# Transposing P for two layers with 40 moving columns and masked evictions

## The chip, the cores and the metric

The kernel runs on one core of a Trainium2 chip, in one launch. The metric is device time in microseconds (us): 2682.25 us is the median of three runs before the change. The engines are TensorE (PE for matmuls, PEld for its weight loads), VectorE (DVE), ScalarE (ACT), GpSimd (POOL) and SyncE (SP).

## The reference

The model is two identical layers, each an attention with a carried memory followed by a gated feed-forward, over 2048 tokens of 576 features, all in bf16:

```
x = x + A(layernorm(x));  x = x + B(layernorm(x));  x = x + A(layernorm(x));  x = x + B(layernorm(x))

A: for each of 64 segments of 32 tokens:
     h = [mem (8 rows), segment (32 rows)]            # 40 rows
     q, k, v = h Wq, h Wk, h Wv                       # 32 heads of 128
     p = softmax(mask(q k^T / sqrt(128)))             # 40 x 40 for each head
     o = (p v) Wo;  mem = o[:8];  out = o[8:]
B: out = (silu(x w1) * (x w3)) w2                     # 4608 wide
```

Each segment needs the memory that the segment before it left, so attention is a chain of 64 steps in each layer.

## The kernel before

**Steps and layers.** The kernel walks 72 steps `t`. At step `t` it does segment `t` of layer 0 and segment `t - 8` of layer 1 (`LAG = 8`). Where both exist (`both(t)`, 56 steps) the two are worked on together: matmuls that use the same weights stream 80 columns, 40 of each layer. The other 16 steps have one layer and 40 columns. `role(t)` is the parity of the step; it decides which layer's columns come first and in which order the rows of keys lie. The feed-forward and the other work of both layers is spread between the steps.

**Groups.** Each step handles the 32 heads in `NG = 4` groups of `GH = 8`; 288 groups in all, 224 of them with two layers. A group runs through these nodes:

- `QK`, `QKt` and their evictions `QKe` (tile `QKT`), then `SC`, the scores of 8 heads. Layer 0's rows stand on partitions 0 to 39, layer 1's on 64 to 103.
- The softmax: DVE adds the mask, takes the maximum and subtracts it, ACT takes the exponential, DVE sums and inverts, and `sm_pb` multiplies and writes P into the tile `PB`. For each head `PB` has the queries on its partitions (0 to 39 and 64 to 103) and 128 columns, one for each row of `V`. `p_at` says which columns a layer's keys take; those of the two layers do not overlap, and the rest is zero.
- `TR` (`ptr`): PE transposes P. `PB[0:104, head]` is the stationary operand, a selection from the identity `ident` the moving one. With two layers the selection has 80 columns, 40 from the partitions of each layer, so 8 heads fill two PSUM banks, 4 heads each.
- `PTe` (`pt_ev`): two evictions, one for each bank, copy the result into the tile `PTS` (128 x 320 each). The planner gives each to ACT or to DVE (`cp` then emits an activation with `Copy` or a `tensor_copy`).
- `pbz` (`pb_zero`): POOL clears `PB` for its next use.
- `PV` (`pv`): for each head the block of `V` is stationary and the head's 80 columns of `PTS` are moving. Then `OTe` evicts into `OT`, and `WO`, `WOt` multiply by the output weights.

There is one `PTS` buffer (`POOLS["pts"]` is 1), two of `PB`, and 8 PSUM banks shared by all.

**Order.** `make_nodes` lists the nodes with durations, dependences and slots; `plan` lays them out. PE's order is not planned: it is the string `ORDER`, one letter for each PE node (`T` is `TR`, `P` is `PV`), whose middle part `FOUR` stands for four steps and is repeated 11 times. In the trace that period is 156.4 us long and holds 16 groups. The order on ACT, DVE and POOL, and which of ACT and DVE takes an eviction (engine `"AD"`), come out of the planned times. Runs of PE nodes share a mode: in `"col"` mode a matmul of 128 weight columns is issued as two of 64, at two column positions of the array, so a `TR` is then 16 matmuls.

**Lines.** All matmuls are recorded at L591, all ACT operations at L594, all DVE operations at L597 and all DMAs of SP at L600, since helpers emit them; POOL's clearing of `PB` is at L1010. Groups in the profile are therefore told apart by their tiles: `bank<-ident,PB` is `TR`, `PTS<-bank` is `PTe`, `bank<-PTS,V` is `PV`.

Of the kernel before, what the change touches and what calls it, by code (L numbers as in the profile page):

```python
# [7 lines left out]
BF = mybir.dt.bfloat16  # L8
F32 = mybir.dt.float32
ACT = mybir.ActivationFunctionType  # L10
ALU = mybir.AluOpType
AX = mybir.AxisListType

P = 128
R64 = 64
# [6 lines left out]
QW = SEG + MEM  # L22
# [5 lines left out]
GH = H // NG  # L28
# [11 lines left out]
def role(t):  # L40

    return (t - LAG) % 2
# [133 lines left out]
def actc(*ns):  # L176

    return sum(max(0.067 + n * 0.000833, 0.19) for n in ns)
# [11 lines left out]
def ew(*ns):  # L190
    return (actc(*ns), dve(*ns))
# [33 lines left out]
class Opt:  # L225

    qk, qkt, sc, tr, pv, wo, wog, vm = 0.0079, -0.0342, 0.0268, 0.1447, 0.0406, 0.2653, 0.0725, 0.1407
# [4 lines left out]
def make_nodes(em, nseg, pools, o=Opt, dma_bw=230e3, load_bw=400e3):  # L232
# [4 lines left out]
    def node(*a, **k):  # L237
        n = Node(*a, **k)
        nodes.append(n)
        return n  # L240

    def banks(n=2):
        return [Slot("bank") for _ in range(n)]
# [22 lines left out]
    b = banks(1)  # L266
# [88 lines left out]
    def step(t):  # L355
        ls = layers_of(t)
        nl = 2 if both(t) else 1
        c80 = 40 * nl
        e = role(t)
        hx = [ht_ready[li, t] for li in ls]  # L360
        hm = ht_mem[t]
        mm80 = max(c80 / 2.4 + 2.5, 25.0) / 1000
        rd = reads_ht.setdefault(t, [])

        for k in () if paired(t) else ((0, 1) if e and both(t) else (0,)):
            last_v[:] = v_nodes("VM", t, k, t + o.vm + 0.01 * k, o.vmt, (lambda k: lambda b, tail: em.vm(t, k, b, tail))(k), em.vm_strips(t, k),
                                hm[:1] + hx + (ld_v if t == 0 else []), hm[1:], {})
        me = steps[t]
        if t == nst - 1:
            last_reads[0].extend(last_v)  # L370
        y = em.ys[t] = Slot("bank", users=2)
        wos, wots = [], []
        for g in range(NG):
            qs, qe = [], []
            for u in (2 * g, 2 * g + 1):
                q = Slot("qkt", users=1)
                b = banks()
                pq = t + o.qk + o.ustep * u
                m_ = node("PE", 32 * mm80, em.qk(t, u, b), deps=hx + hm[:1] + ([ld_h[u // 4]] if t == 0 else []),
                          prio=pq, mode="full", acq=[q] + b, name="QK")  # L380
                n = node("PE", 4 * mm80, em.qk_tail(t, u, b), deps=hx + hm + ([ld_h[u // 4]] if t == 0 else []), prio=pq + o.qkt, mode="row",
                         acq=[q] + b, name="QKt")
                rd += [m_, n]
                me[f"QK{u}"], me[f"QKt{u}"] = m_, n
                for r in (0, 1):
                    qe.append(node("AD", ew(256, 64) if nl == 2 else ew(160), em.qk_ev(t, u, r, q, b[r]), deps=[m_, n], prio=t + o.ustep * u,
                                   rel=[b[r]], name="QKe"))
                qs.append(q)
            s = banks(1)[0]
            sme = Slot("sme")  # L390
            pf = t + o.gstep * g
            sc = node("PE", 8 * (0.0165 * nl if nl == 2 else 0.029), em.scores(t, g, qs, s), deps=qe, prio=pf + o.sc, mode="col" if nl == 2 else "full/col", acq=[s, sme], rel=qs, name="SC")
            a = node("DVE", dve(320), em.sm_add(t, g, s, sme), deps=[sc], prio=pf, rel=[s], name="add")
            m_ = node("DVE", dve(320, 320) + 0.13, em.sm_max(t, g, sme), deps=[a], prio=pf, name="maxsub")
            c = node("ACT", 0.105 + 320 * 0.000833, em.sm_exp(t, g, sme), deps=[m_], prio=pf, name="exp")
            pb = Slot("pb")
            d = node("DVE", dve(320) + 0.2, em.sm_sum(t, g, sme), deps=[c], prio=pf, name="sum")
            w = 0.168 * (4 - e if nl == 2 else 2) + nl * 320 / 960
            pbs = node("DVE", w, em.sm_pb(t, g, sme, pb), deps=[d], prio=pf, acq=[pb], rel=[sme], name="pb")
            pts = Slot("pts")  # L400
            bt = banks()
            tr = node("PE", 8 * mm80, em.ptr(t, g, pb, bt), deps=[pbs], prio=pf + o.tr, mode="full/col", acq=[pts] + bt, name="TR")
            node("POOL", 1.2, em.pb_zero(pb), deps=[tr], prio=pf, rel=[pb], name="pbz")
            pe_ = [node("AD", ew(4 * c80), em.pt_ev(t, g, m, bt[m], pts), deps=[tr], prio=pf, rel=[bt[m]], name="PTe") for m in (0, 1)]
            if paired(t):
                hn = [ht_ready[li, s] for s in (t + 1, t + 2) for li in (0, 1) if (li, s) in ht_ready]
                gb, gd = vg_nodes(t, g, hm[:1] + hx + hn, hm[1:])
                vx_ev["VM", t, g] = vg_out(t, g, gb, gd, R64)
            b = banks()
            ot = Slot("ot")  # L410
            pv = node("PE", 8 * mm80, em.pv(t, g, pts, b), deps=pe_ + vx_ev["VM", t, g] + vx_ev["VX", t - e, g],
                      prio=pf + o.pv, mode="full/col", acq=b + [ot], rel=[pts], name="PV")
            pvs[t, g] = pv
            if paired(t):
                vx_ev["VX", t + 1, g] = vg_out(t, g, gb, gd + [pv], 0)
            ote = [node("AD", ew(4 * c80), em.ot_ev(t, g, ab, b[ab], ot), deps=[pv], prio=pf, rel=[b[ab]], name="OTe") for ab in (0, 1)]
            wo = node("PE", 32 * mm80, em.wo(t, g, ot), deps=ote + ([ld_o[g]] if t == 0 else []), prio=t + o.wo + o.wog * g, mode="full",
                      acq=[y] if g == 0 else [], name="WO")
            wot = node("PE", 4 * mm80, em.wo_tail(t, g, ot), deps=[wo], prio=t + o.wo + o.wog * g, mode="col", rel=[ot], name="WOt")
            if g:  # L420
                wo.after(wos[0])
            if g:
                wot.after(wots[0])
            wos.append(wo)
            wots.append(wot)
            me[f"SC{g}"], me[f"TR{g}"], me[f"PV{g}"], me[f"WO{g}"] = sc, tr, pv, wo
        if t == nst - 1:
            last_reads[1].extend(me[f"{k}{u}"] for u in range(8) for k in ("QK", "QKt"))
        nxt = [li for li in ls if t - LAG * li + 1 < nseg]
        ye = []  # L430
        yo = node("ACT", actc(c80), em.y_odd(t), deps=wots[3:], prio=t - 0.008, name="Yodd")
        if nxt:
            m = 8 * len(nxt)
            ye.append(node("ACT", actc(4 * m), em.y_mem(t, nxt, 0), deps=wos[3:] + wots, prio=t - 0.01, name="Ymem"))
            ye.append(node("DVE", dve(m, m), em.y_mem(t, nxt, 1), deps=[yo] + ye, prio=t - 0.005, name="Ymem"))
        ht_mem[t + 1] += ye
        yts = [node("ACT", actc(*([128] * nl)), em.yts(t, ls, 0), deps=wos[3:] + wots + ye, prio=t + 0.01, rel=[y], name="YTS")]
        yts.append(node("DVE", dve(*([32] * nl)), em.yts(t, ls, 1), deps=[yo] + yts, prio=t + 0.01, rel=[y], name="YTSt"))
        for li in ls:
            yx[li, t - LAG * li] = yts  # L440
# [121 lines left out]
SW = 2 * QW  # L562
# [5 lines left out]
class Emitter:  # L568
# [446 lines left out]
    def ptr(self, t, g, pb, b):  # L1015

        def f(n):
            nq = self.nq(t)
            e = role(t) if nq == SW else 0
            sel = self.T.ident[0:104, R64 * e:R64 * e + QW]  # L1020
            if nq == SW:
                sel = bass.AP(sel.tensor, sel.offset, [list(v) for v in sel.ap][:1] + [[R64, 2], [1, QW]])
            for j in range(GH):
                self.mm(self.bk(b[j // 4])[:, (j % 4) * nq:(j % 4 + 1) * nq], self.T.PB[0:104, pb.i, j, :], sel, True, True)
        return f

    def pt_ev(self, t, g, m, b, pts):
        def f(n):
            w = 4 * self.nq(t)
            self.cp(n, self.T.PTS[:, pts.i, m * w:(m + 1) * w], self.bk(b)[:, 0:w])  # L1030
        return f

    def pv(self, t, g, pts, b):
# [171 lines left out]
def kernel(  # L1205
# [15 lines left out]
    nc = tc.nc  # L1221
# [9 lines left out]
    T = Tiles()  # L1231
    em = Emitter(nc, tc, T, a, nseg)
# [4 lines left out]
    sp = ctx.enter_context(tc.tile_pool(name="state", bufs=1))  # L1237
# [4 lines left out]
    T.WV = wp.tile([P, 9 * H * E // 2], BF, name="WV")  # L1242
    T.WO = wp.tile([P, H, D], BF, name="WO")

    T.ident = sp.tile([P, P + QW], BF, name="ident")

    T.maskb = sp.tile([P, 2, QW], BF, name="maskb")
    T.mhalf = sp.tile([P, 1], F32, name="mhalf")
# [24 lines left out]
    nc.gpsimd.memset(T.ident[:], 0.0)  # L1273
    nc.gpsimd.affine_select(out=T.ident[:, 0:P], in_=T.ident[:, 0:P], compare_op=ALU.not_equal, fill=1.0, base=0,
                            pattern=[[-1, P]], channel_multiplier=1)
    nc.gpsimd.tensor_copy(T.ident[:, P:P + QW], T.ident[:, 0:QW])

    nc.gpsimd.memset(T.maskb[:], 0.0)
    for kd in (0, 1):
        for e in (0, 1):  # L1280
            m = T.maskb[R64 * kd:R64 * kd + QW, e, :]
            x0 = MEM if kd == e else 0
            nc.gpsimd.affine_select(out=m[:, x0:x0 + SEG], in_=m[:, x0:x0 + SEG], compare_op=ALU.is_ge,
                                    fill=MASK_NEG, base=-x0, pattern=[[-1, SEG]], channel_multiplier=1)
# [47 lines left out]
```

## Time and profile before

| | |
|---|---|
| median of three runs | 2682.25 us (2681.96 to 2682.86) |
| profiled execution, first to last instruction | 2684.2 us |
| TensorE clock granted, mean | 0.995 |
| `TR` matmuls, two layers, whole | 1296, busy 73.6 us |
| `TR` matmuls, two layers, half width | 992, busy 30.6 us |
| `PTS` evictions on ACT, 320 elements | 301, mean 436 ns |
| `PTS` evictions on DVE, 320 elements | 147, mean 480 ns |

The profiled execution is one execution; no time of its own is given beside its span, which is 2.0 us above the median of the runs. A row of a group reads: line, engine, operation, tiles written and read, shape, count, then busy time in us and the mean of one in ns, then the idle time of the engine before them and what ended it. Matmuls overlap in the pipeline, so that the mean of one is longer than the step from one to the next.

### The profile page before, as it was taken

Reading aid. Unit: us, or ns where it says so; the run is one execution under the profiler, and the core shown is the slowest. Engines: PE = TensorE matmul, PEld = TensorE weight load, DVE = VectorE, ACT = ScalarE, POOL = GpSimd, SP = SyncE. Lnnn points to the kernel's source line nnn. Section 1 sums busy time; section 2 is a strip of 40 time slices with the busy share of each in tenths; the row PEclk is TensorE's granted clock in tenths of the full one; section 3 lists DMA queues with packets and bytes.
Section 4 is the critical chain, followed back from the end, with each engine's and each line's share of the span. In section 5 each row is a group of like instructions: output and inputs, shape, how many; then the busy total and the mean of one; then the engine's idle time right before and its main releaser. Section 6 shows DMA issues by size and latency. Waiting matters only on the chain.

```text
span 2684.2 us, 136846 instructions
## 1 busy us (share of the span) xinstructions
PE 2621.2 (98%) x60881; PEld 2292.9 (85%) x60933; DVE 2111.8 (79%) x5485; ACT 1346.4 (50%) x3916; POOL 332.2 (12%) x400
## 2 busy tenths in 40 slices
PE   5999999999999999999999999999999999999998
PEld 4888888889888888988888898888889888888887
DVE  4787887887888778787877878787787878687876
ACT  2655554454545455454544545454454545455453
POOL 1111110110111011011101101110110111011110
PEclk8999999999999999999999999999999999999999
DMA  9064524344342434434333443423344342334457
GB/s 319 4 178 118 166 72 125 97 120 118 99 127 84 114 99 119 118 100 126 88 112 97 120 118 100 126 87 113 98 120 118 102 126 82 114 98 130 125 169 256
DMA packets 478178, 322.08 MB, mean 120 GB/s; under 512 B 26024, under 2 KB 467760, under 8 KB 476944
## 3 DMA queue, kind: packets, MB, share of 16 engines
q1 hardware_dynamic: 474048, 305.43, 38.7%
q8 instruction: 477, 7.82, 1.2%
q0 software_dynamic: 3024, 6.93, 0.9%
q10 hardware_dynamic: 512, 0.94, 0.2%
q14 instruction: 117, 0.96, 0.1%
HBM read 308.49 MB, written 2.36 MB: 116 GB/s over the span
## 4 chain that ended last, share of the span: by engine, by line
PE 89%; DMA 3%; DVE 3%; ACT 3%; issue 1%; SPq 1%; ACTq 0%; DVEq 0%
PE bank L591 89%; ACT V L594 1%; SPq L600 1%; DMA W<-in_B_w_dram 1%; DMA W<-in_A_Wk_dram 1%; DVE STAT L597 1%; DVE SME L597 0%; DMA WO<-in_A_Wo_dram 0%; DVE V L597 0%; DVE HTT L597 0%; DVE PB L597 0%; DMA XN<-in_A_x_dram 0%; ACT SME L594 0%; DVE PTS L597 0%; ACT PTS L594 0%
## 5 line engine op out<-in xcount | busy, mean ns | idle before, releaser
L591 PEld LDWEIGHTS <-W 128*128 128x128 bf16 (+2 forms) x32064 | 1267.3, 100 | 118.8 <-issue 55.7
L591 PE MATMUL bank<-HT,W 128*128 128x80 bf16 (+3 forms) x23040 | 807.0, 197 | 14.9 <-ACT HT L594 5.7
L591 PE MATMUL bank<-XTB,W 128*64 128x256 bf16 (+5 forms) x9024 | 664.3, 263 | 4.6 <-DMA W<-in_B_w_dram 3.1
L594 ACT ACTIVATE QKT<-bank 128x256 bf16<-128x256 f32 (+2 forms) x1477 | 343.2, 314 | 362.1 <-PE bank L591 334.1
L1010 POOL MEMSET PB<- 128x1024 bf16 x288 | 273.9, 951 | 1888.4 <-PE bank L591 1537.4
L591 PE MATMUL bank<-OT,WO 128*128 128x80 bf16 (+3 forms) x11520 | 410.9, 198 | 4.6 <-issue 2.0
L591 PEld LDWEIGHTS <-WO 128*128 128x128 bf16 (+1 forms) x11520 | 381.4, 102 | 30.4 <-issue 17.7
L594 ACT ACTIVATE V<-bank 32x512 bf16<-32x512 f32 (+1 forms) x594 | 335.8, 585 | 110.9 <-PE bank L591 104.5
L591 PE MATMUL bank<-WV,HT 128*32 128x512 bf16 (+4 forms) x3628 | 366.2, 383 | 5.5 <-issue 3.2
L591 PE MATMUL bank<-W2C,HTT 128*64 128x288 bf16 (+1 forms) x3040 | 320.1, 287 | 0.8 <-DMA W2C<-in_B_w_dram 0.4
L597 DVE TENSOR_REDUCE STAT<-SME 104x8 f32<-104x320 f32 (+1 forms) x576 | 274.6, 477 | 18.2 <-ACT SME L594 12.4
L597 DVE TENSOR_TENSOR PB<-SME,STAT 40x128 bf16<-40x128 f32 (+4 forms) x912 | 274.9, 335 | 11.3 <-POOL PB L1010 0.5
L594 ACT ACTIVATE HTT<-bank 128x512 bf16<-128x512 f32 (+1 forms) x324 | 177.6, 557 | 196.8 <-PE bank L591 195.5
L591 PEld LDWEIGHTS <-HT 128*32 128x32 bf16 (+4 forms) x3680 | 158.1, 99 | 120.3 <-issue 17.9
L591 PEld LDWEIGHTS <-HTT 128*64 128x64 bf16 (+1 forms) x3104 | 229.4, 104 | 32.1 <-issue 0.6
L597 DVE CAST QKT<-bank 128x128 bf16<-128x128 f32 (+4 forms) x571 | 154.5, 317 | 123.4 <-PE bank L591 122.4
L597 DVE SCALAR_TENSOR_TENSOR XR<-bank,XR 128x288 f32<-128x288 f32 x576 | 239.6, 446 | 13.8 <-PE bank L591 10.9
L597 DVE SCALAR_TENSOR_TENSOR HTT<-HTT,bank 128x512 bf16<-128x512 bf16 (+1 forms) x324 | 202.1, 624 | 56.1 <-ACT HTT L594 51.8
L594 ACT ACTIVATE OT<-bank 128x320 bf16<-128x320 f32 (+1 forms) x425 | 157.0, 405 | 169.5 <-PE bank L591 165.5
L597 DVE TENSOR_TENSOR HTT<-HTT,bank 128x512 bf16<-128x512 bf16 (+1 forms) x324 | 203.6, 628 | 29.0 <-PE bank L591 1.4
L594 ACT ACTIVATE PTS<-bank 128x320 bf16<-128x320 f32 (+1 forms) x395 | 148.2, 404 | 132.3 <-PE bank L591 95.7
L594 ACT ACTIVATE SME<-SME 104x320 f32<-104x320 f32 (+1 forms) x288 | 135.3, 470 | 153.4 <-DVE SME L597 151.1
(61 smaller groups left out, 1837.7 us busy)
## 6 DMA issues: line engine op xcount, KB each, us to landing
W<-in_B_w_dram SPq DMA_DIRECT2D x612, 256.0 KB, 3.7
W2C<-in_B_w_dram SPq DMA_DIRECT2D x306, 288.0 KB, 3.3
W<-in_B_w_dram SPq DMA_DIRECT2D x612, 32.0 KB, 3.3
W<-in_B_w_dram SPq DMA_DIRECT2D x8, 1024.0 KB, 10.5
W<-in_A_Wq_dram SPq DMA_DIRECT2D x9, 512.0 KB, 9.7
WO<-in_A_Wo_dram SPq DMA_DIRECT2D x4, 1152.0 KB, 17.7
XR<-in_A_x_dram POOLq DMA_DIRECT2D x16, 288.0 KB, 3.4
WV<-in_B_w_dram SPq DMA_DIRECT2D x4, 1152.0 KB, 11.3
```

Source lines behind the costliest of these rows:

```text
L591: self.ch("PE", self.nc.tensor.matmul(out, lhsT=lhsT, rhs=rhs, start=start, stop=stop, skip_group_check=True, **k))
L594: self.ch("ACT", self.nc.scalar.activation(*a, **k))
L597: self.ch("DVE", getattr(self.nc.vector, fn_)(*a, **k))
L600: self.ch("SP", self.nc.sync.dma_start(out=out, in_=in_))
L1010: return lambda n: self.ch("POOL", self.nc.gpsimd.memset(self.T.PB[:, pb.i], 0.0))
```

## The change

`TR` no longer selects the two layers into separate columns. Its moving operand is a new constant `fold` of 40 columns, which holds an identity at partitions 0 to 39 and another at 64 to 103. The product has, for each head, 40 columns: column `q` is query `q` of layer 0 plus query `q` of layer 1, on each row of `V`. Since a row of `V` belongs to one layer only, one of the two is always zero.

`PTS` keeps its layout of 80 columns a head. The 8 heads now take 320 columns of one bank, and each of the two evictions reads all of them and writes one half of every head's 80 columns: 8 runs of 40. It multiplies by a 0/1 mask per partition from the new constant `slots`, as the `scale` of the activation on ACT or with `tensor_scalar` on DVE, so that a row of `V` that belongs to the other layer is zero in this half. In steps with one layer the transpose has 40 columns as before, and the two evictions copy a half of the bank each, without a mask.

In the node list `TR` takes one bank with two users in place of two banks, and its planned duration is changed. `fold` and `slots` are built by POOL at the start; a copy of 40 columns behind `ident` goes.

```diff
-            bt = banks()
-            tr = node("PE", 8 * mm80, em.ptr(t, g, pb, bt), deps=[pbs], prio=pf + o.tr, mode="full/col", acq=[pts] + bt, name="TR")
+            bt = Slot("bank", users=2)
+            tr = node("PE", 8 * 0.0258, em.ptr(t, g, pb, bt), deps=[pbs], prio=pf + o.tr, mode="full/col", acq=[pts, bt], name="TR")
             node("POOL", 1.2, em.pb_zero(pb), deps=[tr], prio=pf, rel=[pb], name="pbz")
-            pe_ = [node("AD", ew(4 * c80), em.pt_ev(t, g, m, bt[m], pts), deps=[tr], prio=pf, rel=[bt[m]], name="PTe") for m in (0, 1)]
+            pe_ = [node("AD", ew(4 * c80), em.pt_ev(t, g, m, bt, pts), deps=[tr], prio=pf, rel=[bt], name="PTe") for m in (0, 1)]
...
     def ptr(self, t, g, pb, b):
         def f(n):
-            nq = self.nq(t)
-            e = role(t) if nq == SW else 0
-            sel = self.T.ident[0:104, R64 * e:R64 * e + QW]
-            if nq == SW:
-                sel = bass.AP(sel.tensor, sel.offset, [list(v) for v in sel.ap][:1] + [[R64, 2], [1, QW]])
             for j in range(GH):
-                self.mm(self.bk(b[j // 4])[:, (j % 4) * nq:(j % 4 + 1) * nq], self.T.PB[0:104, pb.i, j, :], sel, True, True)
+                self.mm(self.bk(b)[:, j * QW:(j + 1) * QW], self.T.PB[0:104, pb.i, j, :], self.T.fold[0:104, :], True, True)
         return f
 
     def pt_ev(self, t, g, m, b, pts):
         def f(n):
-            w = 4 * self.nq(t)
-            self.cp(n, self.T.PTS[:, pts.i, m * w:(m + 1) * w], self.bk(b)[:, 0:w])
+            src = self.bk(b)[:, 0:GH * QW]
+            if not self.both(t):
+                w = 4 * QW
+                self.cp(n, self.T.PTS[:, pts.i, m * w:(m + 1) * w], src[:, m * w:(m + 1) * w])
+                return
+            dst = self.T.PTS[:, pts.i, :].rearrange("p (h n) -> p h n", h=GH)[:, :, m * QW:(m + 1) * QW]
+            keep = self.T.slots[:, role(t), m ^ role(t):(m ^ role(t)) + 1]
+            src = src.rearrange("p (h n) -> p h n", h=GH)
+            if n.by == "ACT":
+                self.act(dst, src, ACT.Copy, scale=keep)
+            else:
+                self.v("tensor_scalar", dst, src, keep, None, op0=ALU.mult)
         return f
...
+    nc.gpsimd.memset(T.fold[:], 0.0)
+    for r in (0, R64):
+        nc.gpsimd.affine_select(out=T.fold[:], in_=T.fold[:], compare_op=ALU.not_equal, fill=1.0, base=-r,
+                                pattern=[[-1, QW]], channel_multiplier=1)
+    nc.gpsimd.memset(T.slots[:], 0.0)
+    for e, kd, lo, hi in ((0, 1, 24, 80), (1, 0, 72, 112)):
+        inside, outside = T.slots[:, e, kd:kd + 1], T.slots[:, e, 1 - kd:2 - kd]
...
```

More of the change, by code (lines that the diff above doesn't have):

```diff
@@ L1243 @@
     T.WO = wp.tile([P, H, D], BF, name="WO")
-    T.ident = sp.tile([P, P + QW], BF, name="ident")
+    T.ident = sp.tile([P, P], BF, name="ident")
+    T.fold = sp.tile([P, QW], BF, name="fold")
+    T.slots = sp.tile([P, 2, 2], F32, name="slots")
     T.maskb = sp.tile([P, 2, QW], BF, name="maskb")
@@ L1275 @@
                             pattern=[[-1, P]], channel_multiplier=1)
-    nc.gpsimd.tensor_copy(T.ident[:, P:P + QW], T.ident[:, 0:QW])
+    nc.gpsimd.memset(T.fold[:], 0.0)
[5 more added lines that the diff above has]
+        inside, outside = T.slots[:, e, kd:kd + 1], T.slots[:, e, 1 - kd:2 - kd]
+        nc.gpsimd.memset(inside, 1.0)
+        nc.gpsimd.affine_select(out=inside, in_=inside, compare_op=ALU.is_ge, fill=0.0, base=-lo, pattern=[[0, 1]], channel_multiplier=1)
+        nc.gpsimd.affine_select(out=inside, in_=inside, compare_op=ALU.is_ge, fill=0.0, base=hi - 1, pattern=[[0, 1]], channel_multiplier=-1)
+        nc.gpsimd.tensor_scalar(outside, inside, -1.0, 1.0, op0=ALU.mult, op1=ALU.add)
     nc.gpsimd.memset(T.maskb[:], 0.0)
```

## The prediction

> **What bounds the kernel now.** I read the head of the page and the chain first, then one long window of the steady part.
>
> ```profile
> span 2684.2 us, 136846 instructions
> ...
> PE 2621.2 (98%) x60881; PEld 2292.9 (85%) x60933; DVE 2111.8 (79%) x5485; ACT 1346.4 (50%) x3916; POOL 332.2 (12%) x400
> ...
> PE 89%; DMA 3%; DVE 3%; ACT 3%; issue 1%; SPq 1%; ACTq 0%; DVEq 0%
> ```
> ```profile
> 400.00:2400.00 2000.00, 1990.08 (x44314) 1755.67 (x44361) 1595.57 (x4111) 1010.95 (x2913) 235.41 (x278) 1.00 0.38 109
> 1131.00:1145.00 14.00, 13.95 (x313) 11.59 (x309) 13.12 (x37) 9.76 (x34) 2.45 (x3) 1.00 0.02 4
> ```
> Columns after the window and its length: PE, PEld, DVE, ACT, POOL busy, clock, DMA. Over 2000 us PE is idle for 9.9 us: PE's own instructions set the time, in an order written out by hand, and everything else fits beneath. So a nanosecond off PE's stream is worth a nanosecond, until PE has to wait, and any wait put before PE costs its full length. The second row shows where the cover is thin: where attention is dense DVE has 0.88 us idle in 14.
>
> Next the rows of the touched operations, by shape (busy us, mean ns):
>
> ```profile
> L591 PE MATMUL bank<-ident,PB 104*128 104x80 bf16 x1296 | 73.6, 200 | 0.0
> L591 PE MATMUL bank<-ident,PB 104*64 104x80 bf16 x992 | 30.6, 200 | 0.0
> L591 PE MATMUL bank<-ident,PB 104*128 104x40 bf16 x464 | 21.3, 181 | 0.8 <-DVE PB L597 0.5
> ```
> ```profile
> L594 ACT ACTIVATE PTS<-bank 128x320 bf16<-128x320 f32 x301 | 123.4, 436 | 106.4 <-PE bank L591 74.7 <-DVE XR L597 13.1 <-ACT HTT L594 10.4
> ```
> ```profile
> L597 DVE CAST PTS<-bank 128x320 bf16<-128x320 f32 x147 | 70.6, 480 | 12.4 <-PE bank L591 8.9 <-ACT V L594 2.7
> L597 DVE TENSOR_SCALAR XN<-XR,LNS 128x576 bf16<-128x576 f32 x48 | 28.1, 584 | 3.8 <-POOL LNS L760 3.8
> L597 DVE COPY XN<-XN 128x64 bf16<-128x64 bf16 x64 | 11.6, 182 | 2.2
> ```
> The kernel already transposes with 40 columns in its 64 one-layer groups, so the new price on PE stands in its own trace.
>
> **Taken off PE.** 162 two-layer groups run as 8 whole matmuls. In the timeline their median pitch, start to start, is 36.0 ns; that of the one-layer groups, the same weights with 40 columns, is 25.9. 162 x 8 x 10.1 ns = 13.1 us. The other 62 run as 16 half-width matmuls: pitch 19.6 against 16.4 in the six one-layer groups of that kind, or 17.3 by the half-width 40-column rows of PV; 62 x 16 x 2.2 = 2.2 us. Sum **-15.3 us** (ends -13.5, by busy time with the small end for the halves, and -16.3). PE's order of instructions stays as it was, weight load by weight load; each 156.4 us period of 16 groups loses 1.1 us.
>
> **Put on the path: the evictions.** Four things happen to the pair that empties the transpose into PTS.
> 1. The first eviction now needs all 8 matmuls, not the first 4: in the timeline it starts 0.11 us before the transpose's end, now 0.035 us after it.
> 2. Both read one bank. In the built program the second eviction no longer waits for PE but for its sibling, wherever the two are on different engines: 105 pairs ACT then DVE, 38 DVE then ACT (80 ACT-ACT and one DVE-DVE pair run in turn anyway). Hand-over between ACT and DVE is 33 ns in this trace.
> 3. A DVE eviction turns from CAST into TENSOR_SCALAR with a per-partition pointer. With the planner's own rate for such SBUF rows (`dveh`, 1/1920 us an element) XN<-XR, two pointers, has 584 - 300 = 284 ns of fixed part, the 64-element COPY 182 - 33 = 149: 135 for two pointers. I take 60 for the one, with ends 0 and 120.
> 4. An ACT eviction gets a pointer as its scale; no ACT row here has one. Bounds 0 and 120, by the two DVE pointers; I take 80, DVE's 60 scaled by the fixed parts of an eviction (ACT 436 - 320 x 0.76 = 193 ns, the rate from V's rows of 512 at 585; DVE 480 - 333 = 147).
>
> The Trainium skill ("ScalarE: Activation LUTs", section "What ACT_TABLE_LOAD costs") states about 93 ns for each pointer operand; no run here shows it yet, and the sum below would be 1.6 us larger by it.
>
> Both engines write 320 elements as before; that the output is now in runs of 40 costs nothing, since the ACT rows for QKT in runs of 64 (398 ns for 256) lie within 10 ns of the line of the plain ones.
>
> Who waits: PV is the next user of PTS and stands in PE's fixed stream. I took from the timeline, for all 224 groups, the end of the transpose, the evictions and the start of PV, and moved the evictions by 1 to 4. The period from 1172 to 1328 us stands for the others; only the first two and the last of the 14 differ. Its tight pairs:
>
> ```profile
> 1306.73 0.45 PE L591 MATMUL bank<-ident,PB 104*128 104x80 bf16 x8
> ...
> 1307.33 0.44 ACT L594 ACTIVATE PTS<-bank 128x320 bf16<-128x320 f32 x1
> 1307.66 0.49 DVE L597 CAST PTS<-bank 128x320 bf16<-128x320 f32 x1
> ...
> 1308.17 0.45 PE L591 MATMUL bank<-PTS,V 128*128 128x80 bf16 x8
> ```
> Here ACT and DVE overlap by 0.11 us and PV starts 16 ns after DVE ends. After: ACT ends at 1307.85, DVE runs from 1307.89 to 1308.44, PV at 1308.45: 0.28 us late. The same working gives 0.17 at 1187.91 and 0.17 at 1229.93 (margins of 0.385 us, second eviction 0.54 later), and 0.33 at 1209.10 (DVE then ACT, margin 0.305, ACT 0.80 later). The other twelve pairs keep a margin: up to 9.9 us of other matmuls stand before their PV. So 0.95 us a period, **14.6 us** over 224 groups (6.7 if the masks cost nothing, 21.5 at 120 ns each).
>
> What is queued behind the second eviction on its engine: I followed its lateness down the queue until idle time ate it, and took each PE consumer whose margin was smaller. At 1224.22 DVE reaches a later group's PB 0.21 us too late, at 1295.91 an OT eviction 0.20, at 1298.94 and 1302.64 V evictions 0.23 and 0.03; QKT behind 1209.10 hides under its PV. Counting for each group only the larger of the two, the losses come to **23.1 us** (8.5 and 34.3 at the ends).
>
> One-layer groups gain nothing, but take points 1 and 2 without the mask (27 pairs on two engines): 18 PVs late, **3.1 us** (0 to 3.1, since PE waits in these stretches for other things too).
>
> At nothing: the set-up on POOL (fold, slots: a dozen operations, whose like take 0.1 to 0.3 us) has 6.1 us of idle before POOL's first normalisation to lie in, and would cost what exceeds that; clearing PB on POOL follows the transpose and has 12% load; the bank saved per group frees nothing that PE waits for. The planner moves some 25 OT and 21 V evictions between ACT and DVE, mostly in the ramps; in the period above the pairs keep their engines.
>
> **Sum.** -15.3 + 23.1 + 3.1 = +10.9 us against the profiled execution, whose span of 2684.2 us lies 2 us (0.07%) above the median of the runs; I carry the difference over: 2682.25 + 10.9 = **2693 us**.
>
> **Rivals.**
> - *The masks are free.* If scale and TENSOR_SCALAR cost what the plain evictions do, two-layer losses are 8.5 us; with the ramps absorbed, -16.3 + 8.5 = -7.8: 2674.5 us, faster. It decides in the evictions' own rows: break-even is where losses reach 15.3, at about a quarter to a half of my prices (20 to 40 ns). For it: both engines process 320 elements either way. Against: the 119 ns in the XN rows.
> - *DVE becomes the bound in the dense stretches.* In 1131 to 1145 DVE has 0.88 us idle, and the two pairs in it (1139.56 and 1142.59) make it 0.29 and 0.55 us later, just what there is. Above that it leaves the stretch late for good; if 0.5 us of each period reaches PE, 14 x 0.5 = 7 more: 2700 us. Against: 20% idle elsewhere, and a PE that waits gives DVE time.
> - *PE saves nothing*, the weight load of 128 columns being the limit: +26.2, 2708 us. Against it, the one-layer pitch of 25.9.
>
> **Numbers.** This kernel's measurement can tell about 0.2%, 5.4 us, from no change. My forecast (+5.4 to +16) has 0.42, DVE as the bound 0.18, no saving 0.02: slower 0.62. Free masks has 0.18, which is all of faster. Half-priced masks or well-absorbed waits, landing between -5.4 and +5.4, have 0.20. The range from 2673 (free masks) to 2707 (every bound high: -13.5 + 34.3 + 3.1 = +24) leaves out the two tails, under 2 in 10.
>
> **What would show it.** Right: transposes of 8 matmuls at 0.36 us, not 0.45; ACT's PTS rows near 520 ns and DVE's near 540; DVE's PTS waiting for ACT's; PE waiting for PTS some 10 to 20 us in all, where it is 3.1 now (two rows of waits). Wrong: evictions at 440 and 480 ns, PE's idle time in 400 to 2400 still near 10 us, or a PE saving far from 15.

## The result: 1.6% slower, and the profile after

The changed kernel takes 2724.87 us, the median of five runs (2722.57 to 2730.59), against 2682.25 before: ratio 1.0162, 95% interval 1.0149 to 1.0174. The prediction, +10.9 us with a range up to 2707, had the sign, but the time is 42.6 us longer and lies above the range. The profiled execution is a run of 2723.81 us with a span of 2722.1.

The head of the page of the changed kernel, and its chain by engine:

```profile
span 2722.1 us, 136659 instructions
...
PE 2629.0 (97%) x60933; PEld 2278.8 (84%) x60933; DVE 2115.9 (78%) x5487; ACT 1377.2 (51%) x3914; POOL 333.4 (12%) x411
...
PE 78%; DVE 10%; ACT 6%; DMA 2%; issue 2%; SPq 1%; ACTq 0%; DVEq 0%
```

The long window of the steady part, same columns as before:

```profile
400.00:2400.00 2000.00, 1966.49 (x43657) 1715.67 (x43654) 1573.17 (x4048) 1024.18 (x2864) 232.07 (x275) 1.00 0.37 108
```

PE is now idle for 33.5 of 2000 us, where it was 9.9, and the chain that ended last is PE for 78% of the span and no longer 89%: DVE and ACT have entered it with 16%, from 6. No engine became full: DVE's share went down, from 79 to 78%. These are waits, not work.

The touched operations, by shape:

```profile
L591 PE MATMUL bank<-fold,PB 104*128 104x40 bf16 x1760 | 79.6, 180 | 16.1 <-DVE PB L597 14.7 <-ACT V L594 0.9
L594 ACT ACTIVATE PTS<-bank,slots 128x320 bf16<-128x320 f32 x303 | 151.0, 525 | 163.0 <-PE bank L591 113.7 <-DVE PTS L597 25.9 <-ACT HTT L594 10.2
L597 DVE TENSOR_SCALAR PTS<-bank,slots 128x320 bf16<-128x320 f32 x145 | 78.8, 544 | 46.9 <-ACT PTS L594 43.6 <-PE bank L591 1.4
```

The masks cost 89 ns on ACT (436 to 525) and 64 on DVE (480 to 544); the prediction took 80 and 60. The Trainium skill ("ScalarE: Activation LUTs", section "What ACT_TABLE_LOAD costs") states about 93 ns for a pointer operand of an activation; here it is 89. The last parts of the ACT and DVE rows are new: the evictions wait 25.9 and 43.6 us for each other. The end of the first row shows something that the prediction did not have in this size: PE waits 14.7 us for `PB`, the softmax's output, before its transposes.

PE's own waits, by what ended them (total, times, longest):

```profile
PE bank L591 <- DVE PB L597: 14.7, 29, 0.9
...
PE bank L591 <- ACT V L594: 8.6, 25, 2.1
...
PE bank L591 <- ACT PTS L594: 5.4, 16, 0.7
PE bank L591 <- DVE PTS L597: 4.6, 9, 1.3
PE bank L591 <- DVE HTT L597: 3.8, 12, 0.5
```

Waiting for `PTS` itself is 10.0 us (3.1 before), the lower end of what was forecast. `PB` (0.5 before), `V` (2.1 before) and `HTT` (no such row before), none of which the diff touches, come to 27.1 together.

**A ledger of PE.** These rows miss waits that are shorter than a matmul lasts: one takes some 180 ns while the next starts 26 to 36 ns later, so that a pause of 0.1 us leaves PE busy without a gap (busy time went up from 2621.2 to 2629.0 although 15 us of streaming went). But PE issues the same 60,933 weight loads in the same order in both kernels and in all the variants below. The start of the k-th load in one trace minus its start in the other says where time is lost. Over the ten periods of 156.4 us from 547 us on it repeats to some 10 to 30 ns at nearly every place. A place is named by its time in the period shown in the prediction; a wait is booked at the loads just ahead of it. Lost by PE in one period, in ns, against before (gains of the transposes left out; gain_only, wait_only and old_order are experiments 2, 4 and 1):

| place in before, what waits | predicted | gain_only | wait_only | old_order | after |
|---|---|---|---|---|---|
| 1189.4 PV, pair at 1187.91 | 170 | 0 | 119 | 298 | 297 |
| 1210.6 PV, pair at 1209.10 | 330 | 0 | 301 | 452 | 448 |
| 1228.9 `TR` waits for `PB` | 210 | 90 | 224 | 376 | 399 |
| 1231.5 PV, pair at 1229.93 | 170 | 0 | 108 | 260 | 259 |
| 1256.8 `HT` matmuls | 0 | 0 | 321 | 474 | 464 |
| 1299.3 `V` matmuls, bank freed by an `OT` eviction | 200 | 56 | 178 | 329 | 110 |
| 1300.9 PV | 0 | 0 | 0 | 0 | 244 |
| 1301.3 `WO` matmuls, bank freed by a `V` eviction | 230 | 56 | 56 | 116 | 113 |
| 1304.7 PV, its first matmul, waits for `V` | 0 | 0 | 0 | 44 | 495 |
| 1304.8 the same PV, a later matmul, waits for `V` | 30 | 0 | 119 | 287 | 0 |
| 1306.5 `TR` waits for `PB` | 0 | 0 | 0 | 0 | 988 |
| 1308.2 PV, pair at 1306.73 | 280 | 0 | 284 | 416 | 210 |

In all a period of the changed kernel is 2.66 us longer in the mean of these ten; taken for all 14 that is 37 of the 42.6 us. The transposes themselves give back nearly what was forecast: the loads of `TR` start 14.8 us earlier in sum over the whole run (predicted 15.3). The loss is the waiting.

### The profile page after: what moved, and what is told of

Same layout as the page of the kernel before. It is cut to its first block, busy times and chain, and to the rows that moved or that the text cites. A ratio compares the mean times of both kernels' runs of the same rounds, so it can differ in the third digit from the quotient of the medians.

```text
span 2722.1 us, 136659 instructions
## 1 busy us (share of the span) xinstructions
PE 2629.0 (97%) x60933; PEld 2278.8 (84%) x60933; DVE 2115.9 (78%) x5487; ACT 1377.2 (51%) x3914; POOL 333.4 (12%) x411
## 4 chain that ended last, share of the span: by engine, by line
PE 78%; DVE 10%; ACT 6%; DMA 2%; issue 2%; SPq 1%; ACTq 0%; DVEq 0%
PE bank L591 78%; DVE HTT L597 3%; ACT PTS L594 2%; DVE PTS L597 2%; DVE STAT L597 2%; DVE PB L597 2%; ACT V L594 2%; SPq L600 1%; DVE V L597 1%; DVE SME L597 1%; DMA W<-in_A_Wk_dram 1%; ACT SME L594 1%; DMA W<-in_B_w_dram 1%; DMA WO<-in_A_Wo_dram 0%; ACT QKT L594 0%
## 5 line engine op out<-in xcount | busy, mean ns | idle before, releaser
L594 ACT ACTIVATE QKT<-bank 128x64 bf16<-128x64 f32 (+2 forms) x1476 | 342.5, 314 | 354.9 <-PE bank L591 350.1
L594 ACT ACTIVATE V<-bank 32x512 bf16<-32x512 f32 (+1 forms) x613 | 344.4, 585 | 101.8 <-PE bank L591 94.8
L591 PE MATMUL bank<-WV,HT 128*32 128x512 bf16 (+4 forms) x3680 | 375.8, 381 | 2.1 <-DVE OT L597 0.9
L597 DVE CAST QKT<-bank 128x192 bf16<-128x192 f32 (+4 forms) x572 | 154.5, 316 | 121.2 <-PE bank L591 120.4
L594 ACT ACTIVATE PTS<-bank,slots 128x320 bf16<-128x320 f32 x303 | 151.0, 525 | 163.0 <-PE bank L591 113.7
L594 ACT ACTIVATE OT<-bank 128x320 bf16<-128x320 f32 (+1 forms) x402 | 149.6, 403 | 137.7 <-PE bank L591 132.2
```

The costliest lines, as they stand in the source:

```text
L591: self.ch("PE", self.nc.tensor.matmul(out, lhsT=lhsT, rhs=rhs, start=start, stop=stop, skip_group_check=True, **k))
L594: self.ch("ACT", self.nc.scalar.activation(*a, **k))
L597: self.ch("DVE", getattr(self.nc.vector, fn_)(*a, **k))
```

## The experiments

All times below are compared with the kernel before on the same chip. A difference between two ratios of this section is uncertain by about 0.002, so the ledger, which repeats to some 20 ns a place, decides where ratios are close.

**1. old_order.** The changed kernel with the old plan: `TR` keeps its planned duration and its two slots, but only the first bank is used. Every instruction of ACT and DVE then stands in the order of before.

```diff
-            bt = Slot("bank", users=2)
-            tr = node("PE", 8 * 0.0258, em.ptr(t, g, pb, bt), ..., acq=[pts, bt], name="TR")
+            bt = banks()
+            tr = node("PE", 8 * mm80, em.ptr(t, g, pb, bt[0]), ..., acq=[pts] + bt, name="TR")
```

> The changed kernel laid out by the old plan: the planner is told of two banks and the old duration, so the orders on ACT and DVE and the engine of each eviction are those of before, instruction for instruction. Theory W (the wait of the second eviction for its sibling, whose lateness piles up in the queues of DVE and ACT): the order matters little, 2715 to 2727 us. Theory O (the new order, in which an exponential on ACT now stands behind two evictions of PTS and one of V in the dense stretch): the loss falls to what I predicted or less, 2680 to 2697 us. Theory M (the price of the masks): 2715 to 2727 us, as by W.

Measured: 2720.03 us, ratio 1.0129 (1.0114 to 1.0144). The evictions alone, with no instruction moved, cost most of the loss. The rest, 1.0162 against 1.0129, 9 us, comes with the planner's new order; in the ledger a period is 2.08 us longer than before here, and 2.66 in the changed kernel.

**2. gain_only.** Before with 40 columns, still in two banks; each eviction reads its bank's 160 columns and writes them twice, with no mask.

```diff
-                self.mm(self.bk(b[j // 4])[:, (j % 4) * nq:(j % 4 + 1) * nq], self.T.PB[0:104, pb.i, j, :], sel, True, True)
+                self.mm(self.bk(b[j // 4])[:, (j % 4) * QW:(j % 4 + 1) * QW], self.T.PB[0:104, pb.i, j, :], self.T.fold[0:104, :], True, True)
...
-            self.cp(n, self.T.PTS[:, pts.i, m * w:(m + 1) * w], self.bk(b)[:, 0:w])
+            dst = dst.rearrange("p (h l n) -> p h l n", h=4, l=2)
+            src = src.rearrange("p (h n) -> p h n", h=4).unsqueeze(2).to_broadcast([P, 4, 2, QW])
```

> 40 moving columns into two banks, four heads each, and plain evictions that write each bank's 160 columns twice; the masks are left out, so the layers are not separated. Old plan, no wait between siblings, no pointer. All theories: only the saving on PE is left, 15.3 us less than before, 2667 us (2664 to 2671). If it stays at 2680, PE's saving cannot be had at all, and all of them fall.

Measured: 2675.33 us, ratio 0.9961 (0.9948 to 0.9974): 10.5 us faster, not 15.3. The ledger has the transposes 13.1 us shorter; the rest is given back at places where PE now arrives earlier than what it needs (90 ns at 1228.9, 56 at 1299.3 and at 1301.3).

**3. mask_only.** gain_only with one mask pointer in each eviction (`scale=keep`, or `tensor_scalar` in place of `tensor_copy`).

> As the run with two banks and plain evictions, but every eviction of a two-layer step carries a pointer per partition (one mask for both halves, so the layers are not separated rightly): the price of the masks without the wait. Old plan. Theory W: +3 to +8 us on the run without masks, 2670 to 2675 us. Theory M: most of the loss is here, over 2695 us. Evictions on ACT near 525 ns and on DVE near 544 ns, as in the changed kernel.

Measured: 2681.27 us, ratio 0.9983 (0.9974 to 0.9993). Where both evictions run beside each other, 60 to 90 ns more on each (526 ns on ACT, 540 on DVE) cost 0.0022, some 6 us.

**4. wait_only.** old_order without the masks: one bank, each eviction reads it all, `ACT.Copy` and `tensor_copy` with no pointer.

> The changed kernel with its one bank and its wait between siblings, old plan, but evictions without a pointer (the masks are left out, so the layers are not separated). Theory W: most of the loss is here, 2690 to 2705 us. Theory M: 2667 to 2675 us. Counting each pair by itself, as the prediction did, gives 2682.25 - 15.3 + 8.5 + 3.1 = 2678.6 us; a time well above that shows that the latenesses add up over pairs.

Measured: 2698.18 us, ratio 1.0052 (1.0033 to 1.0071): 0.0091 above gain_only, 24 us. The row of its DVE evictions:

```profile
L597 DVE CAST PTS<-bank 128x320 bf16<-128x320 f32 x147 | 71.3, 485 | 33.6 <-ACT PTS L594 30.9 <-PE bank L591 1.3
```

A plain CAST of the old length, and already 30.9 us of waiting for ACT's eviction of the same bank. The wait is the costly part. Wait and mask together (1.0129 - 0.9961 = 0.0168) cost more than the wait and the mask apart (0.0091 + 0.0022 = 0.0113). The table says why: from wait_only to old_order eight places lose 132 to 179 ns more each, near the 89 + 64 = 153 ns of one pointer on each engine. Evictions one behind the other pay both pointers; beside each other they pay one at most, and often neither.

One rival remains: in the shared bank's layout the two evictions also write interleaved columns of `PTS`, and that could be what makes one wait for the other. The one-layer groups decide. There the changed kernel's two evictions read separate columns of one bank and write separate halves of `PTS`; the rows of DVE's, before and after:

```profile
L597 DVE CAST PTS<-bank 128x160 bf16<-128x160 f32 x34 | 10.6, 318 | 8.9 <-PE bank L591 8.5
```
```profile
L597 DVE CAST PTS<-bank 128x160 bf16<-128x160 f32 x35 | 10.9, 322 | 18.1 <-ACT PTS L594 12.6 <-PE bank L591 5.4
```

In the changed kernel none of the 27 one-layer pairs on two engines overlaps: the second starts 33 ns or more after the first has ended. In before such a pair overlapped by some 0.2 us in the median. So it is the shared bank that makes the second wait.

**5. new_order_no_wait.** mask_only with the planned duration of `TR` that the change brings (8 x 0.0258 us), which gives nearly the order of the changed kernel.

> As the run mask_only (two banks, one pointer in every eviction, so the layers are not separated rightly; no wait between siblings), but planned with the new duration of the transpose, which gives nearly the order of the changed kernel on ACT and DVE. The old order cost 9 us less than the new one where the siblings wait. Theory O (the new order is worse by itself): about 9 us slower than mask_only, a ratio to before near 1.002. Theory W (the order only decides what stands behind a waiting eviction): as mask_only, a ratio of 0.997 to 0.999.

Measured: 2684.02 us, ratio 0.9998 (0.9987 to 1.0008), 0.0015 above mask_only, between the two theories and within the 0.002 that such a difference is uncertain by. In the ledger a period is 0.08 us longer than in mask_only, some 1 us in 14. So the new order by itself costs between 1 and 4 us, and 9 where the evictions wait for each other.

**6. wait_dense_only.** mask_only, with one bank and the changed kernel's evictions only in steps t = 3, 7, 11 ..., where attention is dense.

```diff
+            one = t % 4 == 3        # these groups: all 8 heads into b[0], evictions as in the changed kernel
```

> The wait between siblings in one step of four alone, the dense one at the end of each period; the other three steps empty two banks as in mask_only (masks of one pointer there, so the layers are not separated rightly in those). Old plan. The ledger of PE's stalls puts 0.79 us of the wait's 2.63 us a period into this step. If the stalls of each pair are its own: 14 x 0.79 = 11 us above mask_only, a ratio to before of 1.002 to 1.003. If they need the lateness that the pairs before them left in the queues: 4 us or less above it, a ratio near 0.999.

Measured: 2691.08 us, ratio 1.0023 (1.0009 to 1.0037), 0.0040 or 10.7 us above mask_only. In the ledger its losses at 1299.3 (328 ns), 1304.8 (287) and 1308.2 (415) are those of old_order, and the places outside the stretch lose nothing. So lateness does not pile up from the other steps into this one; the stalls here are this step's own. DVE is not pushed over its limit either: between the same instructions as 1131 to 1145 of before its idle time grew, from 0.88 us of 14.14 to 1.61 of 14.53 in old_order and here.

**7. both_on_act.** The changed kernel with both evictions of each two-layer group planned on ACT, where they run in turn anyway and DVE is relieved.

```diff
-... node("AD", ew(4 * c80), em.pt_ev(t, g, m, bt, pts), ...)
+... node("ACT" if nl == 2 else "AD", (0.525, 0.42)[m] if nl == 2 else ew(4 * c80), em.pt_ev(t, g, m, bt, pts), ...)
```

> The changed kernel with both evictions of every two-layer pair on ACT, one bank, right masks; the planner knows of it and orders the rest anew. No eviction waits for another engine, and DVE is rid of 145 evictions (79 us). Theory W: the loss is gone, 2668 to 2686 us, at or below before. Theory M: the masks are still paid, twice on one engine, 2710 us or more.

Measured: 2703.59 us, ratio 1.0070 (1.0055 to 1.0085). The expectation, 2668 to 2686, missed. In the steady part a period is only 0.25 us longer than before. But one engine in turn is serial too: the tight PVs still lose 100 to 250 ns each, and an `OT` matmul 650. Nearly all the rest is lost near the two ends of the run, outside the four-step pattern; why there was not followed further.

**8. right_masks_two_banks, right_masks_again.** Two banks, and each eviction applies both masks: 4 heads with the 80 columns of each. DVE multiplies by a second tensor operand, the pair of masks read with broadcasting; ACT takes two activations of 160 elements, each with its own pointer. Plan and order as before.

```diff
+            if n.by == "ACT":
+                for l in (0, 1):
+                    self.act(dst[:, :, l, :], src[:, :, l, :], ACT.Copy, scale=self.T.slots[:, role(t), l:l + 1])
+            else:
+                keep = self.T.slots[:, role(t), :].unsqueeze(1).unsqueeze(3).to_broadcast([P, 4, 2, QW])
+                self.v("tensor_tensor", dst, src, keep, op=ALU.mult)
```

> 40 moving columns into two banks of four heads each, old plan, right masks without a shared bank: DVE empties a bank with one tensor_tensor that multiplies 160 columns, read twice, by a mask of two values a partition; ACT takes two activations of 160 elements with one pointer each. No sibling waits. Theory W: near mask_only, a ratio to before of 0.996 to 1.000; the two activations on ACT (estimated 0.39 us each, the second 0.25 us behind, from the 303 ns of the plain 160-element ones and the 89 ns of a pointer) cost some of the gain. Theory M: over 1.005.

> The same kernel as right_masks_two_banks, for a narrower interval beside the two above: 0.9981 again, within 0.0010, so faster than before by a little less than the 0.2% that this kernel's measurement can tell.

Measured: 2679.31 us, ratio 0.9981 (0.9967 to 0.9995), and 2675.59 us, ratio 0.9969 (0.9958 to 0.9980). This version beats both kernels, by some 0.25% over before. Both intervals lie below 1, the first only just (0.05%); in the ledger a period is 0.51 to 0.52 us shorter than before. The second run came out a little better than the 0.9971 that was expected at best.

```profile
L597 DVE TENSOR_TENSOR PTS<-bank,slots 128x320 bf16<-128x320 f32 x147 | 70.5, 480 | 12.3 <-PE bank L591 9.2 <-ACT V L594 0.4
```

The mask as a second tensor costs DVE nothing: 480 ns, as the plain CAST in before and in gain_only, where it reads 160 columns twice as here.

**9. right_masks_told.** The same, with the planner told what these evictions take (0.62 us on ACT, 0.48 on DVE).

> right_masks_two_banks (two banks, right masks: DVE multiplies with a two-value mask operand, ACT takes two activations of 160 elements each) with the planner told what these evictions take (0.62 us on ACT, 0.48 on DVE). If the planner's order is better for knowing the costs, 0.994 to 0.997; if an order chosen by planned times stands apart from what PE feels, as new_order_no_wait says (0.15% slower for a truer duration of TR), 0.998 to 1.001. I take 0.9985.

Measured: 2699.11 us, ratio 1.0057 (1.0044 to 1.0069). A miss: truer durations gave a worse order by 0.9%. PE waits for `PB` again, though for the most part at another transpose (1187.8 in the period shown, 0.9 us in the ledger):

```profile
PE bank L591 <- DVE PB L597: 11.2, 17, 1.1
```

**10. far_pair_only.** mask_only, with one bank and the changed kernel's evictions in a single pair of each period: DVE then ACT, and 9.9 us of other matmuls before its PV. The prediction put nothing on it; old_order loses 474 ns some 5 us behind it.

```diff
+            one = t % 4 == 2 and g == 0
```

> mask_only with the wait in one pair of each period alone: the DVE-then-ACT pair of group 0 in steps t = 2, 6, 10 ..., whose PV has 9.9 us of margin. That pair uses one bank and the right masks; all other pairs keep two banks, and use one mask pointer for both layers, so that only their times count. Order on every engine as before. Theory A (lateness crosses engines: the exponential on ACT stands behind the late pair, DVE's sum waits for it, and the bank that DVE's HTT evictions free comes late): PE loses about 0.47 us in each of 14 periods, at the HT matmuls some 4 us after the pair, 6.6 us in all: ratio 1.0008 (0.9998 to 1.0015), 0.0025 above mask_only. Theory B (the prediction's: only PV and what stands behind the late eviction on its own engine can be late): nothing lost, ratio 0.9983 as mask_only.

Measured: 2681.04 us, ratio 0.9994 (0.9984 to 1.0004), 0.0011 above mask_only; the total lies between the two theories and does not decide. The ledger does: PE loses 471 ns at the `HT` matmuls in every one of the ten periods (467 to 474 for the middle eight), mask_only nothing there; at the other places where PE loses over 40 ns the two differ by 22 ns at most. PE's waits for `HTT`, in far_pair_only and in mask_only:

```profile
PE bank L591 <- DVE HTT L597: 3.7, 13, 0.3
```
```profile
PE bank L591 <- DVE HTT L597: 0.3, 2, 0.2
```

The way from the pair to PE, in the timeline of far_pair_only (start, length, what; in brackets the idle time before and what ended it):

```profile
1244.28 0.55 DVE L597 TENSOR_SCALAR PTS<-bank,slots 128x320 bf16<-128x320 f32 x1
...
1244.86 0.53 ACT L594 ACTIVATE PTS<-bank,slots 128x320 bf16<-128x320 f32 x1 [0.62 <-DVE PTS L597]
1245.29 0.46 ACT L594 ACTIVATE SME<-SME 104x320 f32<-104x320 f32 x1
...
1245.78 0.49 DVE L597 TENSOR_REDUCE STAT<-SME 104x8 f32<-104x320 f32 x1 [0.49 <-ACT SME L594]
...
1248.56 0.69 DVE L597 TENSOR_TENSOR HTT<-HTT,bank 128x512 bf16<-128x512 bf16 x1
...
1249.30 0.88 PE L591 MATMUL bank<-HT,W 128*128 128x80 bf16 x20 [0.31 <-DVE HTT L597]
```

ACT idles 0.62 us for its sibling on DVE. The next group's exponential (`SME`) stands behind it; DVE, which had nothing late of its own, idles 0.49 us for that exponential; everything queued on DVE behind the sum is late; and PE waits for a bank that DVE's `HTT` operation empties. `PTS` is not in the last step at all.

## Why the prediction was wrong, step by step

**Right: what bounds the kernel, and the prices.** PE's stream set the time, and each wait before it cost its length. The transposes became 13.1 (gain_only) to 14.8 us shorter, for 15.3, though only 10.5 of it reaches the time when nothing else changes; the pointers cost 89 and 64 ns for 80 and 60, the hand-over between the two evictions takes 33 to 34 ns for 33. The rivals "masks are free" and "PE saves nothing" fall by these rows; "DVE becomes the bound" falls by DVE's idle time in experiment 6.

**Wrong: "I followed its lateness down the queue".** This is the step that failed most. Lateness was followed on the second eviction's own engine, and only the larger of PV's and the queue's loss was counted for each group. In the traces it crosses: ACT's late eviction delays an exponential, DVE waits for it, and a bank comes free late. Experiment 10 shows it for one pair, priced at zero and costing 0.47 us a period: 5.2 us in the eleven periods in which PE has this wait (13 waits for `HTT`, against 2 in mask_only). At 1299.3 the trace of old_order shows the same kind of way: ACT's exponential waits 1.54 us for DVE (1.33 before), and the `OT` eviction that frees PE's bank stands behind it. At 1228.9 a `PB` was foreseen 0.21 us late, and PE lost 0.38, of which 0.09 appears in gain_only too. For the other places of the queues the way was not followed.

**Wrong in size: the margins of the tight pairs.** The same working that gave 0.17, 0.33, 0.17 and 0.28 us met 0.30, 0.45, 0.26 and 0.42: each 0.09 to 0.14 short, of which a few hundredths are only the transposes' own saving, waited away. For the pair at 1187.91 the relative times show where: in old_order ACT starts 98 ns after the transpose's end (35 were taken) and PV 53 ns after the second eviction (15 were taken, the gap in the pair at 1306.73). The pair at 1306.73 has another reason for part of it: in old_order ACT works on a `V` eviction until 1319.10, 0.22 us after its transposes' end, and was not free earlier although the transposes were 0.09 us shorter. In the changed kernel ACT is free in time there, and the pair costs 0.21 us; it reads, from the timeline:

```profile
1325.43 0.35 PE L591 MATMUL bank<-fold,PB 104*128 104x40 bf16 x8 [0.64 <-DVE PB L597]
...
1325.82 0.53 ACT L594 ACTIVATE PTS<-bank,slots 128x320 bf16<-128x320 f32 x1 [0.62 <-PE bank L591]
...
1326.38 0.55 DVE L597 TENSOR_SCALAR PTS<-bank,slots 128x320 bf16<-128x320 f32 x1 [0.37 <-ACT PTS L594]
...
1326.99 0.45 PE L591 MATMUL bank<-PTS,V 128*128 128x80 bf16 x8
```

Before, ACT and DVE overlapped by 0.11 us; now DVE starts 30 ns after ACT ends.

Together the two steps come to 3.05 us a period in old_order (the sum of its column), against the 1.6 or so of the prediction (23.1 us over 14 periods). A third of the excess lies at the four tight pairs (0.48 us) and two thirds behind the evictions in the queues (0.95 us).

**Wrong: the planner's moves "mostly in the ramps".** Every pair does keep its engines in the period, as was said, but the order around them changes. From the changed kernel's dense stretch, four us ahead of the pair above:

```profile
1321.40 0.53 ACT L594 ACTIVATE PTS<-bank,slots 128x320 bf16<-128x320 f32 x1 [0.83 <-DVE PTS L597]
1321.95 0.59 ACT L594 ACTIVATE V<-bank 64x512 bf16<-64x512 f32 x1
1322.57 0.47 ACT L594 ACTIVATE SME<-SME 104x320 f32<-104x320 f32 x1
...
1322.60 0.46 PE L591 MATMUL bank<-PTS,V 128*128 128x80 bf16 x8 [0.30 <-ACT V L594]
...
1323.08 0.49 DVE L597 TENSOR_REDUCE STAT<-SME 104x8 f32<-104x320 f32 x1 [0.98 <-ACT SME L594]
...
1324.24 1.05 DVE L597 TENSOR_TENSOR PB<-SME,STAT 40x320 bf16<-40x320 f32 x3
```

In before the exponential stood ahead of the `PTS` eviction on ACT; now it stands behind it and behind a `V` eviction. DVE idles 0.98 us for it, `PB` is late, and the transpose at 1325.43 waits 0.64 us; eleven such waits, one a period, are 7.1 of the 14.7 us in PE's first row. The `V` eviction behind the `PTS` eviction is late as well, and the PV at 1322.60 waits for it. At this PV and this transpose (places 1304.7 and 1306.5) the table books 1.4 us a period more than in old_order; 0.18 of it comes back within the same transpose, and most of the rest at the neighbouring places, which lose less. The net is 2.66 - 2.08 = 0.58 us a period, 8 of the 9 us between old_order and the changed kernel.

The sum, by the experiments' ratios: the shorter transposes -10.5 us, their evictions in turn and with masks +45 (0.0168), the order +9; together 43.5, against 42.6 measured. The three ratios add up to 1.0162 by construction, so the sum shares out the loss and is no test of it. The prediction had -15.3, +26.2 and 0; its 3.1 us for the one-layer groups, part of the 26.2, no run measures by itself.

Whether the two evictions could read one bank at once was not tried. The Trainium skill ("PSUM — Partial Sum Buffer", section "PSUM bank collisions raise a hardware error") says that two engines on one bank and the same partitions must be kept apart, reads included. No run here shows a collision; the rows show the wait that keeps the engines apart, and experiment 8 avoids it by giving each engine a bank of its own.

## What to carry to other kernels

Splitting a result by destination instead of by source can turn two parallel evictions into a serial chain: ask first which engines read the same bank, and price the pair as the sum of both lengths, pointers included. Follow a late instruction through everything that waits for it, across engines and through the buffers that it frees, not only down its own queue; a long margin at its own consumer is no cover for its neighbours. And in a kernel whose order comes from a planner, separate the change from the order with one run on the old plan: here truer durations made the order worse twice (the changed kernel against old_order, and experiment 9).

## What the runs showed of the hardware

For 320 elements read from PSUM, a mask per partition costs DVE 64 ns as a pointer and nothing as a second tensor operand that is read with broadcasting: `TENSOR_TENSOR` took 480 ns (right_masks_two_banks and right_masks_again), `TENSOR_SCALAR` 544 (the changed kernel), the plain `CAST` 480 (before).
